# Column tiles 8 to 11 of the state products of batches 0 to 3 from stacked halves, in a fused attention and squared-ReLU kernel

## The chip, the core and the metric

The kernel runs on one core of a Trainium2 chip. The metric is the device time of one execution in microseconds (us); lower is better. Matmuls run on TensorE (PE in the profile, its weight loads PEld), the work beside them on VectorE (DVE), ScalarE (ACT) and GpSimd (POOL). Most transfers are issued by SyncE (SP), some by ScalarE.

## What is computed

For each of 8 batches and 8 heads, 512 tokens and 32 state rows of width 64 read each other by softmax attention; the two results, joined along the rows, go through a feed-forward layer with a squared ReLU.

```python
scores = scale * np.matmul(x, state.transpose(0, 1, 3, 2))       # B 8, H 8, S 512, Ns 32, D 64
a = softmax(scores);   xread = np.matmul(a, state)
scores2 = scale * np.matmul(state, x.transpose(0, 1, 3, 2))
a2 = softmax(scores2); sread = np.matmul(a2, x)
attn = np.concatenate([xread, sread], axis=2)                    # to rows of 512 = 8 heads * 64
h = attn @ w_in                                                  # 512 x 2048
r = np.maximum(h, 0.0); g = r * r
out = g @ w_out                                                  # 2048 x 512
```

## The kernel before

**The products.** For the token rows `xread @ w_in` is not formed in two steps. The kernel first makes, per batch, z = state · w_in (each head's 32 state rows by that head's 64 rows of w_in, for all 2048 columns), and then multiplies the attention weights with z. The 2048 columns are 16 column tiles of 128; two of them make a chunk k (256 columns, k = 0 to 7), four a quarter kq (512 columns, kq = 0 to 3). Heads lie in two groups g of four, each group in two pairs q.

Numbers are split for precision: a float32 operand becomes a high part (a cast on ScalarE to float32r) and a low part (a subtraction on VectorE), and a product is taken as hi·hi + hi·lo + lo·hi, each a matmul of 128x512. The helper `split` (L396) issues both instructions, so they stand at L399 and L404. w_in and w_out come as 64-bit words and are first turned into float32 by `singles` (L408).

**One unit** is a batch and a column tile fc. `up` (L882) multiplies z of the tile with the attention weights into PSUM (`ph`, 6 matmuls), takes the ReLU and the square, and splits the result into `g_hi` and `g_lo`; `down` (L917) multiplies these with the tile's rows of w_out into the four accumulators `po` (12 matmuls). The units run in the order of `PARTS` (L336): batch 0 tiles 0 to 5, batch 1 tiles 0 to 11, batch 0 tiles 6 to 15, batch 1 tiles 12 to 15, then batches 2 to 7 whole and at the end the state rows. So chunk 4 (tiles 8 and 9) is first used by batch 1 in units 14 and 15, chunk 5 in units 16 and 17, and kq = 3 (chunks 6 and 7) from unit 24 on.

**Where z comes from, batches 0 to 3.** Tiles 0 and 1 of batch 0 are made directly (`z_direct`). All else goes through memory and serves four batches at once. There are two ways:

- `z_part(k, g)` (L536): a chunk and a group. Four plain float32 matmuls, contraction 64 (one head each, alternating between the lower and the upper 64 rows of the array), 256 columns, into two PSUM tiles `pz` (L545); two copies on ScalarE into `z_stage` (L528), one store of 512 KB to `zd[k]` on ScalarE's queue. It needs the chunk's two column tiles `wi` and the state `st_z`.
- `z_heads(G, kq, g, q, ...)` (L501): a quarter, a group and a pair of heads, from stacked halves. `w_halves` (L487) lays the high part of a head's 64 rows of w_in above its low part (the two 64-row halves of one tile), by two casts and two subtractions of 64x512; the tile is called `wy` for batches 0 to 3 and lives in the pool tag `raw`. The state's high parts, the same in both halves, and likewise its low parts are the stationary operands. One matmul of 128x512 with the high parts and one with the low ones give a head's product, so four matmuls a call, into two PSUM tiles `py` (L509); two copies (L517) and one store of 512 KB to `zq[G, kq]` on ScalarE's queue. It needs the quarter's four column tiles and the state's halves, made by `z_halves` (L461) from two loads of 256 KB (`sg_raw`) that may begin from unit 8 on. For batches 4 to 7 all z is made in this second way later on (`wz`, `zq_stage`).

`FIRST_KQ = 3` (L319) draws the line: `z_part` makes kq = 0 to 2 (k = 0 to 5), `z_heads` makes kq = 3. `z_fetch(b, k)` (L583) loads a batch's z of a chunk in four pieces of 64 KB on SyncE's queue, and splits it into `z_hi` and `z_lo`. It waits for all stores of its chunk.

The tag `raw` has four buffers. They hold, in turn, the incoming tiles of w_in and w_out (512 KB each), `sg_raw`, the `wy` tiles and the spilled partial sums.

**What sets the order.** No instruction is written in its final place. `Planner` (L50) gets every step with a cost, the buffers it takes, and a due time; due times are passed back from each step to what it needs. It then simulates the engines and takes, on each, the step that can start earliest, and among those the one with the earliest due time. The order that results is issued as it is, and each engine and each queue works through its own list in order. `SHIFTS` (L58) moves the due times of named steps that fall within the first 150 us of the plan. `keep_busy` (L952) adds matmuls on zeros (`idle`) to hold TensorE at its clock, where the plan sees a hole in the first 45 us.

The lines that call the two ways:

```python
    for m in range(2 * FIRST_KQ * NG):
        z_part(*divmod(m, NG))
    z_halves(0)
    for m in range(FIRST_KQ * NG, NFCH // 2 * NG):
        for q in range(NQ):
            z_heads(0, *divmod(m, NG), q, w_halves(0, *divmod(m, NG), q, 0.0), 0.0)
```

Of the kernel before, what the change touches and what calls it, by code (L numbers as in the profile page):

```python
# [49 lines left out]
class Planner:  # L50
# [5 lines left out]
    SLACKS = (2.5,)  # L56
    EARLY = 150.0
    SHIFTS = {  # L58
        ("a_hi", 1): (-7.5, 0.0),
        ("at", 1): (-7.5, 0.12),  # L60
        ("e", 1): (-1.6, 0.19),
        ("g_hi", 1): (-4.1, -0.16),
        ("m", 1): (4.4, 0.0),
        ("out", 1): (0.1, -0.14),
        ("pa", 1): (6.9, 0.0),
        ("po", 2): (3.6, 0.0),
        ("po", 3): (-7.2, 0.22),
        ("po", 7): (-5.3, 0.0),
        ("po", 8): (-0.5, 0.18),
        ("po", 15): (1.4, 0.36),  # L70
        ("po", 18): (-7.2, -0.18),
        ("po", 22): (0.1, 0.0),
        ("po", 23): (-3.4, -0.07),
        ("pz", 1): (-4.8, 0.14),
        ("q", 1): (4.2, 0.0),
        ("q", 3): (-3.9, 0.0),
        ("r", 1): (6.1, 0.0),
        ("st_low", 1): (1.5, 0.18),
        ("wo", 1): (1.1, -0.05),
        ("wo_raw", 1): (-4.5, 0.29),  # L80
        ("wz", 1): (3.2, 0.45),
        ("xt_raw", 1): (-6.0, 0.01),
        ("z_hi", 1): (-0.5, 0.24),
    }

    def __init__(self):
# [203 lines left out]
def memory_attention_then_relu2_ffn(  # L290
# [25 lines left out]
    NT = S // P  # L316
    FW = 256
    NFCH = DF // FW
    FIRST_KQ = 3  # L319
    FPC = FW // P  # L320
    FPQ = 2 * FPC
    GB = P // N
# [26 lines left out]
        r=2, g_hi=2, g_lo=2, os_=3, wof=2, po=4, ph=2, px=2,  # L349
# [5 lines left out]
    def tile_(shape, dtype, name, tag=None):  # L355
        tag = tag or name
        pool = {"po": ps_o, "ph": ps_h, "px": ps_x}.get(tag, sb)
        return Buf(pool, shape, dtype, name, tag, BUFS[tag], hot=tag in ("px", "x_hl"))
# [10 lines left out]
    wi = const.tile([P, NFC, NCC, P], F32, name="wi")  # L369
    wo = [  # L370
        [const.tile([P, FPC, DM], F32R, name=f"{n}{k}") for n in ("wo_hi", "wo_lo")]
        for k in range(NFCH)
    ]
    sd = {
        (b, g): dr.tile([P, S], F32, name=f"sd_{b}_{g}") for b in range(TURNED, PLAIN_X) for g in range(NG)
    }
    zd = [dr.tile([P, NG, HG, FW], F32, name=f"zd_{k}") for k in range(2 * FIRST_KQ)]
    zq = {
        (G, k): dr.tile([P, NG, HG, FPQ * P], F32, name=f"zq_{G}_{k}")
        for G in range(NGB) for k in range(0 if G else FIRST_KQ, NFCH // 2)  # L380
    }
# [70 lines left out]
    st = {}  # L452

    def z_state(G):
        raw = tile_([P, NCC, GB * N], F32, "st_z")
        load(lambda: raw.t.rearrange("p c m -> p (c m)"), lambda: stZ, 256, w=[(raw, 0), (raw, 1)])
        st[G] = raw
# [67 lines left out]
    def z_store(pz, stage, out, keys, part, order):  # L525
        for i in range(2):
            op(
                act(512), lambda e, i=i: nc.scalar.copy(out=part(i), in_=pz[i].t),  # L528
                r=[pz[i]], w=[(stage, i)],
            )  # L530
        load(
            out, lambda: stage.t.rearrange(order), 512,
            r=[(stage, 0), (stage, 1)], w=keys, eng="ACT", issue=0.35, hold=None, land=3.7,
        )

    def z_part(k, g):  # L536
        pz = [tile_([P, NQ, FW], F32, f"pz{i}", "px") for i in range(2)]
        stage = tile_([P, NQ, 2, FW], F32, "z_stage")

        def product(e):  # L540
            for q in range(NQ):
                for i in range(2):
                    own = slice(i * D, (i + 1) * D)
                    cc = g * NQ + q
                    nc.tensor.matmul(  # L545
                        pz[i].t[:, q, :], lhsT=st[0].t[own, cc, :], rhs=wi[own, k * FPC:(k + 1) * FPC, cc, :],
                        start=True, stop=True,
                    )

        op(  # L550
            ("PE", 1.25), product, r=[("wi", k * FPC + i) for i in range(FPC)] + [(st[0], 0), (st[0], 1)], w=pz,
        )
        z_store(pz, stage, lambda: zd[k][:, g].rearrange("p h f -> p (h f)"),
                [("zd", 0, k, g, q) for q in range(NQ)], lambda i: stage.t[:, :, i, :], "p q i f -> p (q i f)")
# [28 lines left out]
    def z_fetch(b, k):  # L583
        raw = tile_([P, NG, FW], F32, "z_raw")
        at = (b % GB) * N
        src = zq[b // GB, k // 2][at:at + N, :, :, (k % 2) * FW:(k % 2 + 1) * FW] if b >= GB or k >= 2 * FIRST_KQ else zd[k][at:at + N]
        for j in range(HG):
# [388 lines left out]
    z_state(0)  # L976
# [5 lines that stand above are left out]
# [3 lines left out]
    spill = {}  # L985
# [96 lines left out]
    for b, lo, hi in PARTS:  # L1082
# [25 lines left out]
        if b == 2 and not z1[0]:  # L1108
            z1[0] = True
            z_halves(1)  # L1110
            for m in range(NFCH // 2 * NG):
                at = begins[2] + m * (begins[GB] - begins[2]) / (NFCH + 2) - 1
# [3 lines left out]
        po = [tile_([P, DM], F32, f"po{t}", "po") for t in range(NT)]  # L1116
        for fc in range(lo, hi):
            k, i = divmod(fc, FPC)
# [4 lines left out]
            z_hi, z_lo = zs[b, k]  # L1123
# [9 lines left out]
            r = [((3 * g, 3 * g + 3), [(z_hi, i), (z_lo, i)] + [(a, g) for a in pairs[b]]) for g in range(NG)]  # L1133
            if u >= 2:
                r = [((0, 3 * NG), r[0][1] + r[1][1][2:])]
# [46 lines left out]
```

## Time and profile before

| what | us |
|---|---|
| median of 3 runs | 668.88 (668.07 to 669.09) |
| profiled execution, device time | 669.25 |
| its span, first to last instruction | 667.5 |
| TensorE busy in it | 660.0 |
| VectorE, ScalarE, GpSimd busy in it | 443.5, 416.5, 90.2 |
| mean granted clock of TensorE | 0.999 |

The span is what the profile shows of an execution; the device time holds 1.75 us more around it. Matmuls are pipelined: a 128x512 matmul shows as about 0.39 us long, but the next begins before it ends, so the cost of a matmul is read from one start to the next. In rows of groups the figures are: line, engine, operation, output <- inputs, shapes, count, then busy time, mean duration in ns, and the idle time of the engine ahead of them. In the answers on one tile the figures are the shortest, the median and the longest duration in ns, and the first and the last start in us.

### The profile page before, as it was taken

How to read it: one execution, taken by the hardware profiler on the slowest of the kernel's cores; microseconds unless marked ns; L12 is line 12 of the kernel's file. 1: busy time of each engine (PE TensorE's matmuls, PEld its weight loads, DVE VectorE, ACT ScalarE, POOL GpSimd, SP SyncE). 2: the span in 40 equal slices, each digit the busy share in tenths (PEclk: the TensorE clock that was granted, in tenths of full speed). 3: DMA queues.
4: the chain of work that ended last, by engine and by line, in shares of the span. 5: the costliest groups of instructions: out<-in, count | busy, mean ns of one | idle time of the engine just before them, and what ended most of it. 6: DMA issues, size and time to landing. Idle time of an engine off the chain costs nothing.

```text
span 667.5 us, 9543 instructions
## 1 busy us (share of the span) xinstructions
PE 660.0 (99%) x3208; PEld 543.9 (81%) x3208; DVE 443.5 (66%) x754; ACT 416.5 (62%) x795; POOL 90.2 (14%) x125
## 2 busy tenths in 40 slices
PE   8999999999999999999999999999999999999997
PEld 6677778888888887888888888888888888988886
DVE  5787887656956798566954694479567945554443
ACT  4998798556668898576643674457556854444331
POOL 1000000033300432021400130013111220000000
PEclk9999999999999999999999999999999999999999
DMA  8989974623623445234130322132223201012101
GB/s 319 353 300 308 274 256 142 234 70 109 221 82 130 143 143 189 68 126 154 53 114 23 104 84 95 31 95 90 96 85 126 64 1 63 1 38 59 32 1 63
DMA packets 43632, 82.41 MB, mean 123 GB/s; under 512 B 7232, under 2 KB 24512, under 8 KB 43584
## 3 DMA queue, kind: packets, MB, share of 16 engines
q1 hardware_dynamic: 38496, 64.38, 29.8%
q10 hardware_dynamic: 5088, 17.44, 6.7%
q8 instruction: 25, 0.41, 0.3%
q14 instruction: 23, 0.19, 0.1%
HBM read 54.00 MB, written 27.79 MB: 123 GB/s over the span
## 4 chain that ended last, share of the span: by engine, by line
PE 92%; DMA 3%; DVE 2%; ACT 2%; issue 1%; SPq 0%; ACTq 0%; DVEq 0%
PE po L930 52%; PE ph L893 28%; PE pr L832 2%; PE pz L509 2%; DMA w_raw<-w_in 2%; PE pq L698 2%; PE pz L545 2%; PE pt L814 1%; DMA wo_raw<-w_out 1%; PE idle L957 1%; PE py L509 1%; PE sq L660 1%; SPq L439 0%; DMA z_raw<-zd 0%; PE pzd L569 0%
## 5 line engine op out<-in xcount | busy, mean ns | idle before, releaser
L930 PE MATMUL po<-wo_hi,g_hi 128*128 128x512 f32 x544 | 213.2, 392 | 0.1
L930 PE MATMUL po<-wo_lo,g_hi 128*128 128x512 f32 x544 | 212.1, 390 | 0.0
L900 ACT ACTIVATE r<-ph 128x512 f32<-128x512 f32 (+1 forms) x144 | 82.7, 575 | 148.9 <-PE ph L893 147.7
L908 DVE TENSOR_TENSOR ph<-ph,r 128x512 f32<-128x512 f32 (+1 forms) x112 | 74.2, 662 | 124.5 <-ACT r L900 124.3
L930 PE MATMUL po<-wo_hi,g_lo 128*128 128x512 f32 x544 | 152.8, 391 | 0.0
L930 PEld LDWEIGHTS po<-wo_hi,g_hi 128*128 128x128 f32 x544 | 102.2, 188 | 22.9 <-ACT g_hi L399 1.1
L930 PEld LDWEIGHTS po<-wo_lo,g_hi 128*128 128x128 f32 x544 | 102.2, 188 | 20.9
L404 DVE TENSOR_TENSOR g_lo<-ph,g_hi 128x512 fp32r<-128x512 f32 (+1 forms) x144 | 94.6, 657 | 33.6 <-ACT g_hi L399 23.6
L930 PEld LDWEIGHTS po<-wo_hi,g_lo 128*128 128x128 f32 x544 | 100.5, 188 | 20.0 <-issue 0.3
L399 ACT CAST g_hi<-ph 128x512 fp32r<-128x512 f32 (+1 forms) x144 | 81.1, 563 | 36.9 <-DVE ph L908 26.3
L893 PE MATMUL ph<-a_hi,z_hi 128*128 128x512 f32 x256 | 101.6, 397 | 0.7 <-DVE g_lo L404 0.7
L893 PE MATMUL ph<-a_hi,z_lo 128*128 128x512 f32 x256 | 99.8, 390 | 0.0
L893 PE MATMUL ph<-a_lo,z_hi 128*128 128x512 f32 x256 | 99.7, 390 | 0.0
L893 PEld LDWEIGHTS ph<-a_hi,z_hi 128*128 128x128 f32 x256 | 48.1, 188 | 12.2 <-DVE g_lo L404 1.3
L893 PEld LDWEIGHTS ph<-a_lo,z_hi 128*128 128x128 f32 x256 | 48.1, 188 | 10.2
L893 PEld LDWEIGHTS ph<-a_hi,z_lo 128*128 128x128 f32 x256 | 48.1, 188 | 9.4 <-issue 0.2
L404 DVE TENSOR_TENSOR z_lo<-z_raw,z_hi 128x512 fp32r<-128x512 f32 x63 | 45.7, 726 | 3.5 <-ACT z_hi L399 3.1
L858 POOL TENSOR_TENSOR sr<-both,low 32x64 f32<-32x64 f32 x64 | 21.6, 337 | 136.5 <-ACT low L850 133.5
L399 ACT CAST z_hi<-z_raw 128x512 fp32r<-128x512 f32 x63 | 39.0, 619 | 1.1 <-DMA z_raw<-zd 0.8
L404 POOL TENSOR_TENSOR xn_hl<-xn_raw,xn_hl 128x512 fp32r<-128x512 f32 x12 | 16.4, 1363 | 171.1 <-ACT xn_hl L399 171.0
L404 DVE TENSOR_TENSOR wz<-wi,wz 64x512 fp32r<-64x512 f32 x32 | 25.0, 780 | 2.2 <-ACT wz L399 1.4
L399 ACT CAST xn_hl<-xn_raw 128x512 fp32r<-128x512 f32 x32 | 19.8, 619 | 9.9 <-PE pr L832 9.0
(152 smaller groups left out, 766.3 us busy)
## 6 DMA issues: line engine op xcount, KB each, us to landing
z_raw<-zq SPq DMA_DIRECT2D x160, 64.0 KB, 2.5
w_raw<-w_in SPq DMA_DIRECT2D x16, 512.0 KB, 6.5
wo_raw<-w_out SPq DMA_DIRECT2D x16, 512.0 KB, 5.1
xn_raw<-xn SPq DMA_DIRECT2D x16, 512.0 KB, 3.3
zq<-zq_stage ACTq DMA_DIRECT2D x16, 512.0 KB, 3.1
xt_raw<-xT SPq DMA_DIRECT2D x15, 512.0 KB, 3.8
zd<-z_stage ACTq DMA_DIRECT2D x12, 512.0 KB, 5.9
z_raw<-zd SPq DMA_DIRECT2D x92, 64.0 KB, 2.5
```

The lines of the kernel that those rows point to most:

```text
L399: act(n, 0.03 if both else 0.0), lambda e: nc.scalar.copy(out=hi(), in_=src()),
L404: lambda e: ENGINE[e].tensor_sub(out=lo(), in0=src(), in1=hi().bitcast(F32)),
L509: nc.tensor.matmul(pz.t, lhsT=halves[G][0](j, g * HG + 2 * q + i), rhs=m.t[:, i].rearrange("p c f -> p (c f)"), start=j == 0, stop=j == 1,)
L545: nc.tensor.matmul(pz[i].t[:, q, :], lhsT=st[0].t[own, cc, :], rhs=wi[own, k * FPC:(k + 1) * FPC, cc, :], start=True, stop=True,)
L660: nc.tensor.matmul(sq.t, lhsT=wide[b].t[:, g].rearrange("p q n -> p (q n)")[:, q * P:(q + 1) * P], rhs=xt.t[:, q, :], start=q == 0, stop=q ...
L698: nc.tensor.matmul(pq.t, lhsT=sp_hl[:, g, q].rearrange("p i n -> p (i n)"), rhs=hl.t[:, i], start=i == 0, stop=i == 1,)
L832: nc.tensor.matmul(pr.t[:, q].rearrange("p i c -> p (i c)"), lhsT=eh.t[:, t, q].rearrange("p i n -> p (i n)"), rhs=hl.t[:, t].rearrange("p ...
L858: nc.gpsimd.tensor_add(out=sr[b // GB][at:at + N, h * D:(h + 1) * D], in0=both.t[i * N:(i + 1) * N, q, i * D:(i + 1) * D], in1=low.t[i * N ...
L893: nc.tensor.matmul(ph.t[:, :width], lhsT=w, rhs=v, start=j == 0, stop=j == len(pairs_) - 1)
L900: act(width), lambda e: nc.scalar.activation(rl.t[:, :width], ph.t[:, :width], AF.Relu),
L908: nc.vector.tensor_mul(out=ph.t[:, :width], in0=ph.t[:, :width], in1=rl.t[:, :width])
L930: nc.tensor.matmul(po[t].t, lhsT=(g[0], g[0], g[1])[j].t[:, t * P:(t + 1) * P], rhs=wo[k][j % 2][:, i, :], start=first and j == 0, stop=la ...
```

## The change

`FIRST_KQ` goes from 3 to 2. `z_part` then makes chunks 0 to 3, and column tiles 8 to 11 (chunks 4 and 5, kq = 2) of batches 0 to 3 go by `w_halves` and `z_heads` into `zq[0, 2]`. The planner's cost for a `z_part` is set from 1.25 to 1.45, and the table `SHIFTS` is replaced by another, so that the whole order of the start is planned anew. The code of the two ways stays as it is.

```diff
     SHIFTS = {
-        ("a_hi", 1): (-7.5, 0.0),
-        ("at", 1): (-7.5, 0.12),
...
-        ("wz", 1): (3.2, 0.45),
-        ("xt_raw", 1): (-6.0, 0.01),
-        ("z_hi", 1): (-0.5, 0.24),
+        ("g_lo", 1): (-0.7, -0.07),
+        ("nm", 2): (7.0, 0.22),
...
+        ("xt_hl", 1): (1.0, -0.14),
+        ("xt_raw", 1): (-0.2, 0.14),
+        ("z_stage", 1): (2.9, -0.4),
     }
...
-    FIRST_KQ = 3
+    FIRST_KQ = 2
...
         op(
-            ("PE", 1.25), product, r=[("wi", k * FPC + i) for i in range(FPC)] + [(st[0], 0), (st[0], 1)], w=pz,
+            ("PE", 1.45), product, r=[("wi", k * FPC + i) for i in range(FPC)] + [(st[0], 0), (st[0], 1)], w=pz,
         )
```

More of the change, by code (lines that the diff above doesn't have):

```diff
@@ L58 @@
     SHIFTS = {
-        ("a_hi", 1): (-7.5, 0.0),
-        ("at", 1): (-7.5, 0.12),
[L61 to L80, printed above, removed]
-        ("wz", 1): (3.2, 0.45),
-        ("xt_raw", 1): (-6.0, 0.01),
-        ("z_hi", 1): (-0.5, 0.24),
+        ("g_lo", 1): (-0.7, -0.07),
+        ("nm", 2): (7.0, 0.22),
+        ("part", 1): (6.4, 0.17),
+        ("po", 1): (1.6, -0.45),
+        ("po", 6): (-1.7, 0.15),
+        ("po", 9): (0.9, 0.37),
+        ("po", 11): (6.9, 0.0),
+        ("po", 16): (0.0, 0.03),
+        ("po", 18): (-1.3, 0.12),
+        ("po", 21): (7.2, 0.06),
+        ("pt", 1): (1.6, -0.24),
+        ("py", 1): (-1.6, 0.0),
+        ("pz", 1): (-4.3, 0.08),
+        ("s", 1): (-1.3, 0.0),
+        ("spill", 1): (-12.5, 0.02),
+        ("st", 1): (-8.8, 0.0),
+        ("wi", 2): (2.7, -0.18),
+        ("wo", 1): (-2.1, 0.17),
+        ("wo_raw", 1): (4.1, 0.0),
+        ("wof", 1): (12.7, 0.05),
+        ("wz", 1): (2.8, 0.34),
+        ("xt_hl", 1): (1.0, -0.14),
+        ("xt_raw", 1): (-0.2, 0.14),
+        ("z_stage", 1): (2.9, -0.4),
     }
```

## The prediction, made before the result

> **What bounds the kernel now.** I read the page first: busy times, the slices, the chain that ended last.
>
> ```profile
> span 667.5 us, 9543 instructions
> PE 660.0 (99%) x3208; PEld 543.9 (81%) x3208; DVE 443.5 (66%) x754; ACT 416.5 (62%) x795; POOL 90.2 (14%) x125
> ...
> PE 92%; DMA 3%; DVE 2%; ACT 2%; issue 1%; SPq 0%; ACTq 0%; DVEq 0%
> ```
>
> TensorE is busy for 99% of the span and 92% of the chain lies on it. So the end is set by three sums: the matmuls that are issued, the idle matmuls that fill holes, and the few real stalls. An engine beside it counts only where it makes one of the last two. The waits of TensorE and the idle fillers say how large those are.
>
> ```profile
> PE sq L660 <- DMA xt_raw<-xT: 1.0, 1, 1.0
> PE idle L957 <- DVE warm L366: 1.0, 1, 1.0
> PE ph L893 <- DVE g_lo L404: 0.7, 1, 0.7
> PE pz L509 <- ACT zq_stage L517: 0.3, 1, 0.3
> PE pzd L569 <- DVE wi L431: 0.3, 1, 0.3
> ...
> L957 PE MATMUL idle<-warm x128: 219/219/314, 1.0 to 37.7; 128*128 128x128 bf16 x128
> ...
> 11.93 1.79 PE idle L957 x32
> 14.78 1.67 PE idle L957 x28
> ```
>
> All stalls together are 3.3 us. The last two rows are from the chain (start, us, what): the largest fillers behind the first scores, 3.5 us. No filler starts after 37.7 us. From there on TensorE is fed almost without a break, and a microsecond of matmul taken out there is a microsecond of the end, as long as what comes next is ready.
>
> **The products that go.** `z_part` runs for chunks k = 0 to 5 and two groups, twelve times; the change leaves k = 0 to 3. The trace shows the twelve as 96 records, eight each. I read two of them, with their neighbours, in the timeline (start, us, instruction):
>
> ```profile
> 57.51 0.40 PE L930 MATMUL po<-wo_hi,g_lo 128*128 128x512 f32 x1
> 57.84 1.13 PE L545 MATMUL pz<-wi,st_z 64*128 64x256 f32 x8
> 58.90 0.50 PE L893 MATMUL ph<-a_hi,z_hi 128*128 128x512 f32 x1
> 59.24 0.40 PE L893 MATMUL ph<-a_hi,z_lo 128*128 128x512 f32 x1
> ...
> 78.22 0.39 PE L930 MATMUL po<-wo_lo,g_hi 128*128 128x512 f32 x1
> 78.53 1.13 PE L545 MATMUL pz<-wi,st_z 64*128 64x256 f32 x8
> 79.60 0.50 PE L893 MATMUL ph<-a_hi,z_hi 128*128 128x512 f32 x1
> 79.94 0.40 PE L893 MATMUL ph<-a_hi,z_lo 128*128 128x512 f32 x1
> ...
> 112.96 0.39 PE L893 MATMUL ph<-a_lo,z_hi 128*128 128x512 f32 x1
> 113.19 0.39 PE L509 MATMUL py<-wy,wo_hi 128*128 128x512 f32 x1
> ...
> 113.87 0.39 PE L509 MATMUL py<-wy,wo_lo 128*128 128x512 f32 x1
> 114.10 1.07 PE L930 MATMUL po<-wo_hi,g_lo 128*128 128x512 f32 x4
> ```
>
> Durations overlap, so I count from start to start. Between the third and the fourth of the last group lie two more `py`. A 128x512 matmul takes one place of (114.10 − 112.96) / 5 = 0.228 us. From 57.51 to 59.24 are 1.73 us, from 78.22 to 79.94 are 1.72; each holds two ordinary places (0.46) beside the `z_part`, which therefore costs 1.27 us: 1.06 inside, and about 0.1 on each side, where the matmul before it and the one behind it take 0.33 and 0.34 instead of 0.23. Four go: 5.08 us. They are the last four of the twelve, after 57 us, where TensorE is fed without holes.
>
> **The products that come.** `z_heads` of batches 0 to 3, now also for quarter kq = 2: two groups by two pairs, each with two tiles of two matmuls: 16 matmuls 128x512, as the `py` rows. 16 × 0.228 = 3.65 us. Net on TensorE: 3.65 − 5.08 = **−1.43 us**.
>
> A rule of the Trainium skill speaks against that saving. By "FP8 and Floating Point Precision" (TensorE Precision Notes) a true FP32 matmul makes four passes, and by "TensorEngine Tiling" (Theoretical Speedup) a contraction of 64 gains up to two by row tiling; so the four 256-column products would stream 4 × 256 × 4 / 2 = 2048 columns, as many as four of 512, and the net would be nothing. The rows above show 1.06 against 0.91 us inside, and by "TensorEngine Tiling" (Key Properties) a change of tiling mode drains the engine, which agrees with the 0.33 and 0.34 at the edges.
>
> **What comes beside TensorE.** Each of the four new `z_heads` needs `w_halves` first: two casts on ScalarE, two subtractions on VectorE.
>
> ```profile
> L399 ACT CAST wy<-wi x8: 602/617/622, 92.2 to 108.6; 64x512 fp32r<-64x512 f32 x8
> L404 DVE TENSOR_TENSOR wy<-wi,wy x8: 685/687/689, 93.0 to 109.7; 64x512 fp32r<-64x512 f32 x8
> L517 ACT COPY yq_stage<-py x8: 579/590/606, 101.5 to 121.4; 128x512 f32<-128x512 f32 x8
> L439 ACTq DMA_DIRECT2D zq<-yq_stage x4: 326/326/333, 103.3 to 122.0; - x4
> ...
> L528 ACT COPY z_stage<-pz x24: 572/590/612, 14.8 to 86.1; 128x512 f32<-128x512 f32 x24
> ...
> 40.00:104.00 64.00, 63.18 (x296) 48.88 (x294) 54.54 (x99) 55.62 (x107) 2.34 (x2) 1.00 0.81 271
> 104.00:150.00 46.00, 46.00 (x215) 38.20 (x214) 28.25 (x48) 30.26 (x59) 7.67 (x12) 1.00 0.46 150
> ```
>
> Eight casts are 4.9 us and eight subtractions 5.5 us, both new. The copies out of PSUM are eight before and after, 0.59 us each; the stores are four of 512 KB before and after, on the same queue (ACT's), and `z_fetch` reads the same 64 KB pieces, from another tensor. So the addition beside TensorE is 10.4 us of work on two engines. In the stretch from 40 to 104 us (columns of the windows: stretch, length, PE, PEld, DVE, ACT, POOL, clock, DMA, GB/s) VectorE is busy 54.5 of 64 and ScalarE 55.6, together 17.9 us free: it fits, but fills 58% of the room. From 104 to 150 both are idle for a third, and what is not urgent can go there: `w_halves` and the loads for kq = 3, whose last store is issued only at 122 us, and the last tiles of w_out. I price the 10.4 us at nothing on the path. Its cover is the matmul stream. If that cover is gone the bounds are, on one side, nothing, and on the other a stall of the kind seen, 0.7 us for `ph` behind `g_lo`, twice: 1.4 us. I keep nothing, since one such stall in 64 us at 86% is what the trace shows.
>
> Two kinds of step move. The stacked state (`sg_raw`, two loads of 256 KB, then two casts and two subtractions) was loaded at 77 us and must come ahead of kq = 2; 512 KB at the 271 GB/s of the row are 1.9 us by which the loads behind it on SP's queue, weights of the next quarter among them, land later. And four more tiles `wy` pass through the four buffers of the tag raw, in which the weight loads stand too; a load that waits there for a `py` product holds back every later load on SP's queue, z pieces included. The trace has that wait already:
>
> ```profile
> SPq L439 <- PE py L509: 7.6, 3, 4.8
> ```
>
> The nearest row bounds it: 7.6 us of queue wait for four `wy` tiles, of which TensorE felt none. With eight tiles in a tighter place it may feel some; that is a rival below. A planner cost of 1.45 in place of 1.25 issues nothing.
>
> **The sum.** The profiled execution took 669.25 us with its span of 667.5; the median of the runs shown is 668.88, 0.37 below. 669.25 − 1.43 = 667.82 for that execution, and **667.4** for a median. About 0.2% (1.34 us) is what a measurement of this kernel can tell from no change: the forecast is barely beyond it, 667.54 being the edge.
>
> **Rival 1: the new order fills the early holes.** Every step of the first 150 us gets another due time, and the start has 3.5 us of fillers and 3.3 us of stalls to win. The 1.0 for the first x and the 1.0 for the memset of the idle operand stand at the very start and stay; of the other 4.8 a better order may win half: 667.4 − 2.4 = 665.0. For it: nothing in the sixteen column tiles forces the holes at 12 to 17 us once z is in hand. Against: the memory queue runs at its fullest there, and any new order can lose as much as it wins.
>
> **Rival 2: z of chunk 4 comes too late (slower).** Before, chunk 4 needed column tiles 8 and 9 and two `z_part`; now both 4 and 5 need tiles 8 to 11, the stacked state, four `w_halves`, eight `py` tiles and four stores.
>
> ```profile
> 57.02 0.68 DVE L431 SCALAR_TENSOR_TENSOR wi<-w_raw,wi 128x512 int32<-128x512 int32 x1
> 86.74 0.33 ACTq L439 DMA_DIRECT2D zd<-z_stage  x1
> 93.48 0.39 PE L893 MATMUL ph<-a_hi,z_hi 128*128 128x512 f32 x1
> 104.46 0.39 PE L893 MATMUL ph<-a_hi,z_hi 128*128 128x512 f32 x1
> ...
> 87.48 0.69 DVE L404 TENSOR_TENSOR z_lo<-z_raw,z_hi 128x512 fp32r<-128x512 f32 x1
> 103.07 0.69 DVE L404 TENSOR_TENSOR z_lo<-z_raw,z_hi 128x512 fp32r<-128x512 f32 x1
> ...
> zd<-z_stage ACTq DMA_DIRECT2D x12, 512.0 KB, 5.9
> zq<-yq_stage ACTq DMA_DIRECT2D x4, 512.0 KB, 3.2
> ```
>
> The last of tiles 8 to 11 is ready at 57.7 (first row). Units 14 and 15, the first users of chunk 4, begin at 93.5 (unit 16, of chunk 5, at 104.5); with 1.4 us saved ahead of them, 92.1. So the whole chain has 34.4 us. For kq = 3 it took, from the first cast (92.2) to the landing of the last store (122.0 + 3.2), 33 us; then comes the fetch and split, for chunk 5 from the store's landing (86.7 + 5.9) to the end of `z_lo` (103.8), 11.1 us. Together 44: at that pace the unit would be 9.7 us late. But that pace was leisurely, since kq = 3 was not due until later; at three quarters of it nothing is late. That is the point from which it decides. Halfway the delay is 4.8 us, of which a held-back `down` of 12 matmuls (12 × 0.228 = 2.7) could fill part: 2.1 us of stall and, with the saving inside, 667.4 + 2.1 = 669.5; with the same stall a second time, before chunk 5, 671.6. I take 670.5. For it: 0.7 us lay between the end of `z_lo` of chunk 5 (103.8) and its use at 104.5, so this place is already tight. Against: chunk 4's z was split (87.5 to 88.2) 5 us ahead of its use, and the due times pull the chain forward.
>
> By "TensorE: Matmul & The Clock Gate" (Part 1) a TensorE idle for about 3.4 us falls to half clock, which would make a long stall dearer; the clock column here is 1.00 throughout, and no run here shows it.
>
> **Rival 3: the saving is given back.** Two more stalls of 0.7 us under the 10.4 us of new conversions, or the rule on passes being right in substance: 667.4 + 1.4 = 668.8, no change. For it, 86% busy on both helpers; against, the room after 104 us, and for the rule the 1.27 us of the rows.
>
> **How the numbers follow.** Forecast (start as good as before to within 1 us): 0.42, which falls about evenly on both sides of the edge, 0.23 faster and 0.19 within 0.2%. Rival 1: 0.22, faster. Rival 2: 0.20, slower. Rival 3: 0.16, of which 0.04 for the rule on passes, within 0.2%. So faster 0.45, within 0.2% 0.35, slower 0.20. The range reaches down to rival 1 at 664.8 and up past rival 2 to 671.0; outside lie the far ends of both, about 0.18 in all.
>
> **What would show it.** In the changed profile: 64 records of `pz` L545 instead of 96, 32 of `py` L509 instead of 16, 16 casts and 16 subtractions of `wy`; the last `z_part` before about 60 us; start-to-start distances of 0.228 at the `py`. If the forecast is right, TensorE's stalls and fillers sum to what they do now, within 1 us, and no wait of `ph` names a `z_lo` or a z transfer. Rival 2 shows as a wait of `ph` behind `z_lo` or `z_hi` between 85 and 110 us, with fetches queued on SP behind `py`. Rival 1 shows as fewer than 128 idle matmuls or shorter stalls before 45 us. The forecast is wrong if the products cost other than 1.27 and 0.228, or if fillers and stalls move by more than the 1.4 us that the products give.

## The result and the profile after

The changed kernel takes 675.20 us (median of 5 runs, 672.78 to 675.40) where the kernel before takes 668.88 (668.07 to 670.26): ratio 1.0087, 95% interval 1.0071 to 1.0103. It is slower by about 6 us, outside the forecast range. Three of its five executions, at a mean granted clock of 0.997, take 675.20 to 675.40 us, and the two at 0.999 and 1.0 take 672.78 and 673.01. The profiled execution is one of the three: it took 675.37 us, and its span is 673.4; the 1.97 us around the span were 1.75 before, so 0.2 us of the difference does not show in the profile.

First the page of the changed kernel: span, busy times, and the shares of the chain that ended last.

```profile
span 673.4 us, 9529 instructions
PE 663.0 (98%) x3196; PEld 546.4 (81%) x3196; DVE 450.6 (67%) x764; ACT 419.9 (62%) x800; POOL 91.5 (14%) x126
...
PE 84%; ACT 7%; DMA 5%; DVE 2%; issue 1%; SPq 0%; ACTq 0%; DVEq 0%
```

Twelve matmuls net are gone, as intended (64 records of `pz` from `z_part` for 96, 32 of `py` for 16, 4 more idle ones), and yet TensorE shows 3.0 us more busy time. TensorE's share of the chain fell from 92% to 84%; ScalarE's rose from 2% to 7%. Next TensorE's waits:

```profile
PE po L929 <- ACT os__871 L945: 2.6, 1, 2.6
PE idle L956 <- DVE warm L365: 1.0, 1, 1.0
PE ph L892 <- DVE g_lo L403: 0.9, 1, 0.9
PE po L929 <- ACT g_hi L398: 0.7, 1, 0.7
```

and the stretches of the prediction with the middle one cut finer (columns: stretch, length, PE, PEld, DVE, ACT, POOL, clock, DMA, GB/s):

```profile
40.00:104.00 64.00, 60.25 (x267) 47.41 (x266) 56.87 (x100) 56.31 (x108) 3.98 (x3) 0.97 0.70 240
...
60.00:80.00 20.00, 17.39 (x70) 13.78 (x69) 18.35 (x31) 18.07 (x35) 0.00 (x0) 0.91 0.78 283
```

From 40 to 104 us TensorE is busy for 60.25 us instead of 63.18, its clock is 0.97 instead of 1.00, and the two helpers have 14.8 us free instead of 17.9. Between 60 and 80 us they have 3.6 us free of 40; in the kernel before, they had 7.3, and TensorE was busy throughout:

```profile
60.00:80.00 20.00, 20.00 (x95) 15.67 (x94) 17.18 (x34) 15.48 (x33) 0.00 (x0) 1.00 0.92 308
```

The longest wait is new: `po` behind `os__871`, a copy on ScalarE. TensorE's timeline at that place (start, us, instruction; in brackets the idle time and what ended it):

```profile
59.34 0.39 PE L929 MATMUL po<-wo_hi,g_hi 128*128 128x512 f32 x1
...
59.79 0.39 PE L929 MATMUL po<-wo_hi,g_lo 128*128 128x512 f32 x1
...
61.83 0.39 PE L929 MATMUL po<-wo_hi,g_lo 128*128 128x512 f32 x1
64.83 0.80 PE L929 MATMUL po<-wo_hi,g_hi 128*128 128x512 f32 x1 [2.61 <-ACT os__871 L945]
65.42 0.63 PE L929 MATMUL po<-wo_lo,g_hi 128*128 128x512 f32 x1
65.85 0.63 PE L929 MATMUL po<-wo_hi,g_hi 128*128 128x512 f32 x1
```

And ScalarE's over the same time:

```profile
58.90 1.14 ACT L398 CAST wo_hi<-sg_raw 128x512 fp32r<-128x512 f32 x2 [1.71 <-DMA sg_raw<-stH]
59.95 0.59 ACT L899 ACTIVATE r<-ph 128x512 f32<-128x512 f32 x1
61.38 0.67 ACT L416 ACTIVATE wo_raw<-wo_raw 128x512 f32<-128x512 f32 x1 [0.85 <-DMA wo_raw<-w_out]
61.95 0.60 ACT L398 CAST wy<-wi 64x512 fp32r<-64x512 f32 x1
62.46 0.57 ACT L398 CAST g_hi<-ph 128x512 fp32r<-128x512 f32 x1
62.94 0.59 ACT L899 ACTIVATE r<-ph 128x512 f32<-128x512 f32 x1
63.55 0.61 ACT L398 CAST wy<-wi 64x512 fp32r<-64x512 f32 x1
64.19 0.59 ACT L945 COPY os__871<-po 128x512 f32<-128x512 f32 x1
```

This is the hand-over of the accumulators. The first part of batch 0 ends with the `down` of 59.34 to 61.83; batch 1's first `down` may not write `po` before batch 0's sums are copied out. The first accumulator is finished by 60.2 (its third matmul starts at 59.79), but ScalarE works through its list in order, stands behind two transfers that have not landed (1.71 and 0.85) and two of the new `wy` casts, and copies only at 64.19. TensorE starts again 3.00 us after its last start, and then its matmuls stand 0.43 us apart instead of 0.228: for about 3.4 us it runs at half clock.

In the kernel before, 5.4 us lay between the last `down` of batch 0 and the first of batch 1: the `z_part` at 57.84, twelve `ph`, and a second `z_part`, of which the timeline shows

```profile
57.25 0.59 ACT L946 COPY os__815<-po 128x512 f32<-128x512 f32 x1
...
61.84 1.13 PE L545 MATMUL pz<-wi,st_z 64*128 64x256 f32 x8
62.90 0.50 PE L930 MATMUL po<-wo_hi,g_hi 128*128 128x512 f32 x1
```

The change takes both products away, and the new order puts the `ph` ahead of the last `down`, so that nothing is left between.

To see the whole, I took every distance of TensorE from one start to the next, subtracted the ordinary place of its kind (the median in the kernel before; a `z_part` 1.06), and summed the rest by stretch of the profiled execution. This is arithmetic on the trace, not a view; all in us. The rest of the span, 5.4 us in both, lies ahead of TensorE's first start and behind its last.

```
kernel     span   places  fillers  lost in 0-40  40-60  60-80  80-120  120-300  from 300
before     667.5  644.7     8.9         3.1      1.2    0.4     1.5      1.2      1.0
after      673.4  644.1    10.1         2.4      0.7    4.5     2.9      2.3      1.0
```

The products give 0.6 in places and 0.8 more in the edges of the four `z_part`, which stood under "lost". The fillers take 1.1 more, the stretch from 60 to 80 us 4.1 (some 1.6 of it the half clock), that from 80 to 120 us 1.3, and short waits after 160 us 1.1.

### The profile page after: what moved, and what is told of

Read it like the earlier page. It is cut to its first block, busy times and chain, and to the rows that moved or that the text cites. A ratio compares the mean times of both kernels' runs of the same rounds, so it can differ in the third digit from the quotient of the medians.

```text
span 673.4 us, 9529 instructions
## 1 busy us (share of the span) xinstructions
PE 663.0 (98%) x3196; PEld 546.4 (81%) x3196; DVE 450.6 (67%) x764; ACT 419.9 (62%) x800; POOL 91.5 (14%) x126
## 4 chain that ended last, share of the span: by engine, by line
PE 84%; ACT 7%; DMA 5%; DVE 2%; issue 1%; SPq 0%; ACTq 0%; DVEq 0%
PE po L929 48%; PE ph L892 26%; DMA w_raw<-w_in 2%; PE pr L831 2%; PE pz L508 2%; PE pq L697 1%; PE pz L544 1%; PE pt L813 1%; DMA wo_raw<-w_out 1%; PE idle L956 1%; ACT wz L398 1%; ACT r L899 1%; DMA xn_raw<-xn 1%; ACT wy L398 1%; DMA zq<-yq_stage 1%
## 5 line engine op out<-in xcount | busy, mean ns | idle before, releaser
L907 DVE TENSOR_TENSOR ph<-ph,r 128x512 f32<-128x512 f32 (+1 forms) x114 | 75.5, 663 | 121.4 <-ACT r L899 121.1
L892 PEld LDWEIGHTS ph<-a_lo,z_hi 128*128 128x128 f32 x256 | 48.2, 188 | 10.2
L892 PEld LDWEIGHTS ph<-a_hi,z_lo 128*128 128x128 f32 x256 | 48.3, 189 | 10.1 <-DVE z_lo L403 0.8
L403 DVE TENSOR_TENSOR z_lo<-z_raw,z_hi 128x512 fp32r<-128x512 f32 x63 | 47.9, 761 | 3.5 <-ACT z_hi L398 3.2
```

The source lines that it names most:

```text
L403: lambda e: ENGINE[e].tensor_sub(out=lo(), in0=src(), in1=hi().bitcast(F32)),
L892: nc.tensor.matmul(ph.t[:, :width], lhsT=w, rhs=v, start=j == 0, stop=j == len(pairs_) - 1)
L907: nc.vector.tensor_mul(out=ph.t[:, :width], in0=ph.t[:, :width], in1=rl.t[:, :width])
```

## The experiments

Each was timed beside runs of the kernel before on the same chip; e1 to e4, e5 to e8, e9 to e12, e13 to e15 and e16 to e18 each share one set of these, and the ratios are to that set. The theories: **T**, the prediction's, TensorE's sum sets the end. **H**: between 57 and 107 us the work in the in-order lists of ScalarE and VectorE sets the pace as much as TensorE does. **A**: the loss is the one uncovered hand-over. **C**: the late load of the stacked state is at the root of it. **R** was formed later: the landings of weight loads, for which those lists wait, set the pace. The letters in the expectations are not all the same: B there, the overfull helpers, is H here; C there is wider in most places, lists in order that wait for transfers, of which R is a part; and in e3, e4 and e11 A is the order at large.

### The products alone, in the order of before

```diff
         def product(e):
+            if k >= 4:
+                for i in range(2):
+                    for q in range(NQ):
+                        nc.tensor.matmul(pz[i].t..., lhsT=wo[0][q][:, i, :P], rhs=wo[0][0][:, i, :],
+                                         start=q == 0, stop=q == NQ - 1)
+                return
```

e15 has the same edit without the loop over `q`: two matmuls in each of the four places instead of four.

> The kernel before, with its order untouched: only the matmuls of the four z_part calls of chunks 4 and 5 are replaced, at their places, by four 128x512 float32r matmuls each, on other data (z of chunks 4 and 5 is then not the reference's). Theory (a z_part costs 1.27 us, four 128x512 matmuls 0.91): 4 x 0.36 = 1.4 us less, 667.4. Rival (only streamed columns count, 2048 against 2048): no difference, 668.9. If the second holds, the exchange itself was mis-priced by 1.4 of the difference between forecast and result.

> The kernel before, in its order, with each z_part of chunks 4 and 5 replaced by two matmuls of 128x512 where e1_exchange had four (z of these chunks not the reference's): 1.27 - 0.46 = 0.81 us of TensorE less in each of four places, 3.25 in all, and nothing else touched. If TensorE's sum sets the end after 37.7 us, as the prediction said: 668.75 - 3.25 = 665.5, 0.995. If the helpers' lists set the pace between 57 and 107 us, the time that is taken out comes back as waits of po and ph, as in e1: 0.999 to 1.004.

Measured: e1 670.37 (668.57 to 672.66), ratio 1.0032 [1.0018, 1.0047]; e15 670.62 (667.53 to 672.64), 1.0026 [1.0009, 1.0044]. Taking 1.43 us or 3.25 us out of TensorE, and nothing else, gives nothing; the time rises by about 2 us (what part half clock has in that is told at the end). T falls. The waits of e15, and its timeline at the longest:

```profile
PE ph L900 <- DVE g_lo L404: 3.4, 2, 2.1
```

```profile
78.79 0.39 PE L900 MATMUL ph<-a_lo,z_hi 128*128 128x512 f32 x1
81.32 0.50 PE L900 MATMUL ph<-a_hi,z_hi 128*128 128x512 f32 x1 [2.15 <-DVE g_lo L404]
81.66 0.49 PE L900 MATMUL ph<-a_hi,z_lo 128*128 128x512 f32 x1
81.94 0.63 PE L900 MATMUL ph<-a_lo,z_hi 128*128 128x512 f32 x1
```

The `g_lo` that it waits for, and in the kernel before the same `g_lo` and the same `ph`:

```profile
80.58 0.69 DVE L404 TENSOR_TENSOR g_lo<-ph,g_hi 128x512 fp32r<-128x512 f32 x1
...
80.31 0.69 DVE L404 TENSOR_TENSOR g_lo<-ph,g_hi 128x512 fp32r<-128x512 f32 x1
81.09 0.46 PE L893 MATMUL ph<-a_hi,z_hi 128*128 128x512 f32 x1
```

In the kernel before, TensorE came to this `ph` at 81.09, and `g_lo` had ended at 81.00: ready in time by 0.1 us. In e15 TensorE comes early and waits for a `g_lo` that ends at 81.27, no earlier than it did before.

### Room for the helpers

The kernel before without the conversions of tiles 8 to 15 of w_out (e7), and the same with the cheaper products of e1 (e8).

```diff
+        first = len(plan.ops)
         singles(lambda: wf.t, lambda: raw.t, [raw], [wf])
         split(lambda: wo[k][0][:, i, :], lambda: wo[k][1][:, i, :], lambda: wf.t, DM, ...)
+        if fc >= 8:
+            for o in plan.ops[first:]:
+                o.run = leave_out
...
-                            rhs=wo[k][j % 2][:, i, :], start=first and j == 0, stop=last and j == 2,
+                            rhs=wo[k if k < 4 else 0][j % 2][:, i, :], start=first and j == 0, stop=last and j == 2,
```

> The kernel before, its order untouched, with the conversions of the tiles 8 to 15 of w_out left out (about 3 us each on ScalarE and VectorE together; the transfers stay, and those products read tile 0 and 1 of w_out instead). It serves as the base of the next run. Both theories: the wait of 0.7 us at 95.5 us, and little else, goes: 667 to 668.

> The same, with the products of chunks 4 and 5 exchanged as in the first experiment. Theory C (the exchange does save 1.4 us of TensorE, and it was lost because ScalarE's and VectorE's lists, waiting for transfers of weights, hold TensorE up between 67 and 98 us): without these conversions the saving reaches the end, 1.0 to 1.5 us less than the run before it. Rival D (the exchange is worth nothing on TensorE, or memory transfers of z hold it): within 0.4 us of the run before it.

Measured: e7 668.30, ratio 0.9995 [0.9984, 1.0006]; e8 667.29, ratio 0.9983 [0.9972, 0.9994]. Between them lie 1.0 us of the 1.43; drawing new sets from the twelve executions of each puts it between 0.5 and 1.7. So the exchange does save TensorE time, and it arrives, at least in good part, once the helpers have less to do; with their full lists (e1) none does.

### The new conversions

The changed kernel without the eight casts and eight subtractions of `wy` for kq = 2.

```diff
+            if (G, kq) == (0, 2):
+                for o in plan.ops[-2:]:
+                    o.run = leave_out
...
-                        rhs=m.t[:, i].rearrange("p c f -> p (c f)"), start=j == 0, stop=j == 1,
+                        rhs=wo[0][0][:, i, :] if (G, kq) == (0, 2) else m.t[:, i].rearrange("p c f -> p (c f)"), ...
```

> The changed kernel with the 8 casts and 8 subtractions of wy for column tiles 8 to 11 left out (the products read another tile, so z of these tiles is not the reference's); order and all else as they are. Rival B (ScalarE and VectorE overfull by these 10.4 us): the waits of TensorE between 55 and 110 us, 4.4 us and a stretch at half clock, fall to 1.5 us or less, and the time falls by 4 us or more, to 671 or less. Theory C (lists in order that wait for transfers): the two casts ahead of the first copy of po go, 1.2 us, but the wait for w_out and the stacked state stays: the time falls by 1 to 3 us, to 672 to 674.

Measured: 671.80 (669.27 to 674.53), ratio 1.0045 [1.0030, 1.0060] for 1.0087: the 10.4 us of conversions cost 2.8 us of the end, with an uncertainty of about 1.4. Some 1 us of it is half clock that comes less often, in 3 of 12 executions instead of 3 of 5: among those at full clock the medians are 670.9 (ratio 1.0035) and 672.9 (1.0060), 1.7 us apart. This is less than the 4 us that was expected if overfull helpers were all of it. The loss from 80 to 120 us falls from 2.9 to 0.6; the wait at the hand-over stays:

```profile
PE po L939 <- ACT os__868 L955: 2.3, 1, 2.3
```

### The hand-over

e2 moves the three copies of `po` on ScalarE ahead of the `wo_raw` and `wy` work in its list. e9 moves the `up` of the next unit on TensorE behind the last `down`, so that six matmuls more lie there, and `r`, the copies and `g_hi` ahead of the casts of the stacked state. e10 is e9 with the sixteen `wy` conversions of kq = 3 about 8 us later. e5 is e2 with the stacked state loaded some 20 us earlier (issued at 32.3 us instead of 53.1), into storage of its own.

```diff
         log = min(plans)[2]
+        copies = [x for x in log if x[3].kind[0] == "os_"][:3]
...
+        moved = [downs[0], copies[0], downs[1], copies[1], downs[2], copies[2], downs[3]]
...
+        front = [up, first("DVE", "z_lo"), relu, downs[0], square, copies[0], hi, downs[1],
+                 copies[1], lo, downs[2], copies[2], downs[3]]
...
+            while wys and wys[0][0] + 8.0 <= x[0]:
+                log.append(wys.pop(0))
...
+        early = [x for x in log if x[2] == "SP" and x[3].bufs and x[3].bufs[0].name == "sg_raw"]
+        log = log[:at] + early + [x for x in log[at:] if not any(x is y for y in early)]
```

(`moved` is of e2 and e5, `front` of e9 and e10, the loop of e10, `early` of e5.)

> The changed kernel, with one edit of its order: the first three copies of the accumulators of batch 0 on ScalarE stand ahead of the wo_raw step and the two wy casts instead of behind them. Theory A (the copies came late because ScalarE's list waited for a transfer and for the new casts; po of batch 1 had to wait 2.6 us and TensorE then ran 3.4 us at half clock): that wait is gone or under 1 us, the clock stays at 1.00 there, and the time falls by 3 to 4.5 us, to 671 to 672. Rival B (ScalarE and VectorE are simply overfull from 55 to 110 us by the 10.4 us of new conversions): the wait returns a few us later at another place, and the time falls by less than 1.5 us, 674 or more.

> The changed kernel with the copies of po moved up, and the stacked state loaded some 15 us earlier into storage that is free until the reads of x, so that ScalarE's casts of it find their data (1.4 us of waiting before). Theory C (between 57 and 105 us ScalarE and VectorE work through lists in order, and each wait of theirs for a transfer reaches TensorE): TensorE's wait behind g_hi at 62 us falls from 1.5 to under 0.5 us, and the time falls by 1 to 2.5 us against the run with the copies moved up alone (674.1), to 671.6 to 673. Rival B (the two engines are simply overfull there): no change beyond 0.7 us, the wait moves on.

> The changed kernel with the hand-over from batch 0 to batch 1 given cover again: the first up-product of unit 6 stays ahead of the last down of batch 0, that of unit 7 goes behind it, and ScalarE makes the three copies of po, with the relu and cast of unit 6 between them, ahead of the casts of the stacked state. Theory A2 (the stall of 2.8 us and the 3.4 us at half clock come from TensorE having nothing between the last down of batch 0 and the first of batch 1): the wait for the copies and the half clock go, 1.36 us of up-products lie in between, and 3 to 4.5 us are saved, 671 to 672. Rival B (ScalarE and VectorE are behind by that much anyway): TensorE waits as long for g_hi or py within the next 15 us, less than 1.5 us saved.

> The same, and the 16 conversions for column tiles 12 to 15 (the third to fifth use of wy, not needed before 110 us) stand about 8 us later in the lists of ScalarE and VectorE. By the run without wy conversions the waits between 88 and 107 us, 2.4 us in the changed kernel, hang on the load of these two engines. Theory B (load): these waits fall to under 1 us and 1.5 us are saved against the run before it, 669.5 to 671. Theory C (waits for transfers of weights in those lists): no change beyond 0.7 us. If both edits work, the time comes near that of the kernel before.

Measured: e2 674.13, ratio 1.0087 [1.0072, 1.0103]; e5 677.40, 1.0131 [1.0110, 1.0152]; e9 673.70, 1.0079 [1.0066, 1.0092]; e10 674.25, 1.0087 [1.0073, 1.0101]. The wait for the copy goes, and others take its place. First e2, then e9:

```profile
PE po L937 <- ACT g_hi L406: 2.1, 2, 1.5
PE py L516 <- ACT yq_stage L524: 1.4, 2, 0.9
```

```profile
PE py L524 <- ACT yq_stage L532: 1.5, 2, 1.0
...
PE ph L908 <- DVE g_lo L419: 0.9, 1, 0.9
```

The loss between 60 and 80 us stays at 4.6 us in e2, 4.5 in e5, 4.3 in e9 and e10 (4.5 in the changed kernel). In these four profiles there is no half clock in it: other waits have come in the place of the one. In e9 the row is

```profile
60.00:80.00 20.00, 17.16 (x71) 12.46 (x70) 18.30 (x31) 17.90 (x34) 0.00 (x0) 1.00 0.79 282
```

Among executions at full clock e2 stands at 1.0089 and e9 at 1.0073 (four of five each), no better than the changed kernel at 1.0060 (two of five). A falls in its simple form: the one wait can be taken away, its time cannot. H, too, expected more of e10, 1.5 us, and it gained nothing over e9. C found no support: e5 lies about 3 us above e2, where C expected 1 to 2.5 less and H no change; but e5 loses 0.8 us at unit 4 already, where its early loads stand in the way of others, so it doesn't settle C alone.

### Which order, which line

Two tables, no table (`SHIFTS = {}`), and both values of `FIRST_KQ`; the planner's cost of a `z_part` is 1.45 with the new table and 1.25 otherwise. e3 has the old table and e12 none, at `FIRST_KQ = 2`; e4 has the new table and e11 none, at 3.

```diff
-    FIRST_KQ = 3
+    FIRST_KQ = 2
...
-    SHIFTS = {
-        ("a_hi", 1): (-7.5, 0.0),
...
+    SHIFTS = {}
```

> Only FIRST_KQ goes to 2; the planner's cost of 1.25 and the table of shifts stay those of the kernel before, and the order is planned from them. Theory A (the loss is in how this order fell out, a hand-over without cover, not in the stacked products): another order with the same products, whose time may lie on either side, 666 to 674, and where it loses, the waits of TensorE name other places than the copies of po. Rival B (the stacked products of chunks 4 and 5 cost the early stage more than it has): again 672 or more, with waits of TensorE above 4 us between 55 and 110 us.

> The new table of shifts and the cost of 1.45, but FIRST_KQ stays 3: the products of the kernel before in yet another order. Theory A (an order decides, not the products): a time that differs from 668.9 by more than 1 us either way, likely longer, as this table was not made for these products. Rival B (the products decide): within 1 us of 668.9.

> The kernel before with an empty table of shifts: its products, in the order that the planner gives by itself. Theory A (orders that were not picked lose several us through waits): 672 to 690. Rival (the order matters little): within 1.5 us of 668.5.

> FIRST_KQ at 2, an empty table and the planner's cost at 1.25: the pair of the run before. If the stacked products themselves fit the early stage, it lies within 3 us of that run on either side; if they load the stage beyond what it has, it is 3 us or more slower.

```
median, us (ratio)    old table           no table          new table
FIRST_KQ = 3          668.88 (1)          677.34 (1.0130)   676.88 (1.0123)
FIRST_KQ = 2          689.21 (1.0324)     685.33 (1.0253)   675.20 (1.0087)
```

An order tuned for the other structure is no better than none (676.88 beside 677.34, 689.21 beside 685.33); e3 lies far above the 666 to 674 that was expected of it. A table of its own is worth 8.5 us to `FIRST_KQ = 3` and 10.1 to 2. With no table the change costs 8.0 us, with each structure's own 6.3. So a table made for the old structure is not the reason for the loss: the change is slower in both fair pairs. But each cell is a single order, and orders of one structure lie 8 to 14 us apart, so the pairs don't say how much of the 6 us is structure and how much the order that was found; that a better order exists for `FIRST_KQ = 2` is not excluded.

### Do the costs add up?

The changed kernel with the edits of e6 and e9 together (e13), and with that of e7 too (e14).

> The changed kernel with both single edits that gained at all: the eight casts and eight subtractions of the stacked tiles of kq = 2 left out (the products read a tile of w_out in their place, so z of chunks 4 and 5 is not the reference's), and the hand-over from batch 0 to batch 1 covered by an up unit, as in e9_cover. If the two costs are separate and add up as they did one by one (1.0087 to 1.0045, and 1.0087 to 1.0079): 1.0037, 671.2 us. If the stalls that e9 still had between 60 and 80 us come from the load of the two helper engines, they go with the conversions, and all that the profile of the change put down to stall and half clock (4.4) comes back as well: 675.2 - 4.4 - 2.8 = 668.0, 0.999. Rival: the stalls there belong to the order itself and to late transfers: 671 to 673, with a loss of about 4 us between 60 and 80.

> The same, and the conversions of column tiles 8 to 15 of w_out left out too (down uses tiles 0 and 1 there, so the output is not the reference's): the fewest conversions on ScalarE and VectorE of all kernels here. If these two engines' load between 57 and 107 us is what kept the 1.43 us of TensorE from arriving, this kernel is about as far below the kernel before as the exchange without these conversions was (0.9983, 667.3), or 1.4 below at best (0.9979). If the new order itself costs what is left (fillers and stalls of the first 40 us, stalls between 60 and 80 us), it stays above: 1.001 to 1.004.

Measured: e13 670.17 (669.38 to 672.09), ratio 1.0023 [1.0012, 1.0035]; e14 669.44, ratio 1.0016 [1.0005, 1.0027]. The two edits give 0.64%, 4.3 us, together, where one by one they gave 0.42 and 0.08. None of the twelve executions of e13 is at half clock, which is part of it. The stretch that was worst in the changed kernel, now in e13 (its profiled execution is the longest of its runs):

```profile
60.00:80.00 20.00, 19.51 (x85) 15.52 (x84) 14.46 (x25) 15.32 (x29) 0.00 (x0) 1.00 0.84 291
```

TensorE is busy for 19.5 of the 20 us, not 17.4, and the helpers have 10.2 us free, not 3.6: with the conversions gone, the cover holds there. From 80 to 104 us this execution of e13 still has TensorE idle for 2.3 us, of which 1.5 are two waits of `ph` behind `g_lo`. e14 has hardly a stall left between 40 and 104 us,

```profile
40.00:104.00 64.00, 63.09 (x292) 50.53 (x291) 50.29 (x88) 50.42 (x96) 3.99 (x3) 1.00 0.73 246
```

and still stands at 1.0016, where e8, with the same products in the old order and the same conversions of w_out left out, stands at 0.9983. That difference, 0.33% or 2.2 us, goes with the new order: fillers of 10.1 us for 8.9, and 1.1 us more lost between 120 and 300 us.

So the 0.87% can be walked: cheaper products with helpers that have room −0.17% (e8), the new order +0.33% (e14), the conversions of w_out +0.07% (e13), the sixteen new conversions and the bare hand-over +0.64%; each step is uncertain by 0.1 to 0.2%, so the 0.07 is not told from nothing. The last step holds the half clock too: among executions at full clock the changed kernel is at 1.0060, so some 0.3 of the 0.64 is half clock.

### What holds the lists: work or landings

The kernel before (e16), e1 (e17) and e15 (e18) with loosened loads: the stacked state in storage of its own, so that one tile fewer passes the tag raw, and three spill stores behind two loads of w_in on SyncE's queue instead of between them.

```diff
+        spills = [x for x in queue if x[3].kind[0] == "spill"][1:4]
...
+        log = head + spills + tail
...
+            raw.make = lambda: sr[0]
```

> The kernel before with its loads loosened and nothing else: the stacked state of batches 0 to 3 is loaded into storage of its own (that of the state rows' sums, unused until the end), so one tile fewer passes through the four buffers of the tag raw, and three spill stores go behind two loads of w_in on SyncE's queue instead of between them. Conversions, products and the orders of all engines stay. In the profiles so far unit 12 starts 5.5 us after a w_in tile has landed (75.50 and 81.09 here, 76.30 and 81.84 in e1, 75.78 and 81.32 in e15) and unit 15 7.0 us after a w_out tile (89.58 and 96.60; 90.88 and 97.88; 91.11 and 98.10). Theory R, the landings of weight loads set the pace: both landings come 1 us or more earlier, the stall of 0.86 before unit 15 goes, 667.9 or a little less, 0.998 to 0.999. Theory H, the helpers' load sets it: 1.000.

> The same loosened loads with the cheaper products of e1_exchange (z of chunks 4 and 5 not the reference's). All conversions are made. Theory R: what e1 lost (1.0032) behind late landings goes, and the 1.43 us of TensorE arrive at least in part: 0.996 to 0.999. Theory H: as e1, 1.002 to 1.004, since the helpers have the same work.

> The same loosened loads with the products of e15_half_product, 3.25 us less of TensorE (z of chunks 4 and 5 not the reference's). Theory R: the start of unit 12 is still 5.5 us after a landing, but the landing is 1 us or more earlier, and that of the w_out tile 2 us or more; so at least 1 to 2 of the 3.25 us arrive: 0.994 to 0.999. Theory H: as e15, 1.001 to 1.004.

Measured: e16 668.99 (668.12 to 673.00), ratio 1.0020 [1.0004, 1.0036]; e17 669.68, 1.0026 [1.0009, 1.0042]; e18 671.66 (670.16 to 673.50), 1.0052 [1.0035, 1.0069]. The times are nearer to H than to R, and e18 fits neither. The starts in the profiles say why (us of the span; the landing is that of the w_out tile whose conversion stands in ScalarE's list ahead of the `g_hi` that unit 15 waits for):

```
             unit 12  unit 14   landing   unit 15   landing to unit 15
before        81.09    93.48     89.58     96.60      7.02
e1            81.84    93.80     90.88     97.88      7.00
e15           81.32    94.39     91.11     98.10      6.99
e16           81.03    93.20     89.14     96.30      7.16
e17           81.16    92.94     89.29     96.47      7.18
e18           80.57    91.90     89.53     96.58      7.05
e7 (left out) 81.23    93.40       -       95.73       -
e8 (left out) 80.74    92.61       -       94.88       -
```

The loosened loads bring the w_in tile forward (it landed at 75.5 to 76.3, now at 73.3 to 74.3), and unit 12 no longer waits: e18 is 1.57 us ahead of the kernel before at units 13 and 14. But the w_out tile lands at 89.1 to 89.5, at most 0.4 ahead of the kernel before, and unit 15 begins 7.0 to 7.2 us after it in all six, while unit 14 begins anywhere between 91.9 and 94.4. ScalarE in the kernel before,

```profile
89.67 0.66 ACT L424 ACTIVATE wof<-wo_raw 128x512 int32<-128x512 uint8 x1 [0.87 <-DMA wo_raw<-w_out]
...
92.25 1.27 ACT L399 CAST wy<-wi 64x512 fp32r<-64x512 f32 x2
...
95.26 0.56 ACT L399 CAST g_hi<-ph 128x512 fp32r<-128x512 f32 x1
```

and in e18, where TensorE comes earlier:

```profile
89.61 0.68 ACT L434 ACTIVATE wof<-wo_raw 128x512 int32<-128x512 uint8 x1 [0.77 <-DMA wo_raw<-w_out]
...
92.24 1.26 ACT L409 CAST wy<-wi 64x512 fp32r<-64x512 f32 x2
...
95.23 0.57 ACT L409 CAST g_hi<-ph 128x512 fp32r<-128x512 f32 x1
```

The same list at the same times: a landing, then 5.6 us of instructions one behind the other, eight of them conversions, then `g_hi`, then `g_lo` on VectorE, then TensorE. So H and R are each a part of it: the landing sets when the list goes on, and the conversions in it set how long it takes. Where the conversions are left out (e7, e8), unit 15 follows unit 14 by 2.3 us and a saving on TensorE passes through. In e18 the wait is 2.25 us, unit 16 begins 1.58 us late, half clock follows in the profile, and all six executions have a mean clock below 0.9985: more time is lost than was taken out.

No version here beats the kernel before with all of its work done.

## Why the prediction was wrong, point by point

**The products: right.** The twelve `z_part` of before sum to 13.00 us from start to start inside, the eight of after to 8.52, 1.08 and 1.07 each; the added `py` stand 0.227 apart, the last four 0.23 to 0.26. The rule of the Trainium skill by which both ways would stream alike ("FP8 and Floating Point Precision", TensorE Precision Notes, with "TensorEngine Tiling", Theoretical Speedup) leaves no saving; e8 against e7 measured one of 1.0 us, so the rows decide.

**"A microsecond of matmul taken out there is a microsecond of the end": this step failed.** The page's 99% and the chain's 92% were read as one bound. In the kernel before, TensorE and the helpers' lists were level at several places (0.1 us at 81.09, a stall of 0.86 at 95.5), and the `z_part` stood there as cover that needed little from the helpers. The clause "as long as what comes next is ready" was written, but not applied to the places where the products stood: the `g_lo` that ended at 81.00 for a `ph` at 81.09 was in the trace.

**"I price the 10.4 us at nothing on the path": failed too.** They cost 2.8 us by e6, some 1 us of it as half clock. The upper bound of 1.4 was too low: 86% busy over 64 us says that there is room, not where, and a list that stands behind a landing cannot use the room that it has. The stall of 0.7 us behind `g_lo` was read as the size that such a thing may have; it was the sign that the lists were already the bound there.

**The cover named for it, "the matmul stream", was what the change took away.** At the hand-over 5.4 us of matmuls became none, at a price of 2.77 us of stall and about 1.6 of half clock in the profiled execution. Putting six matmuls back there (e9) did not win that time; it did so only together with fewer conversions (e13).

**The order.** Fillers and losses before 40 us went together from 12.0 to 12.5 us: rival 1, holes filled, did not come. The 2.2 us between e14 and e8 lie in fillers and at places after 120 us that the prediction did not look at.

**Rival 2 had the right sign and mostly the wrong place.** Its mark, a wait of `ph` behind `z_lo` between 85 and 110 us, is there and 0.2 us long. Unit 14, the first to use chunk 4, begins at 100.58 instead of 93.48, and that is mostly by the plan: unit 13 is 2.3 us late by then (91.73 for 89.40), and 32 matmuls of held-back `down` stand between the two instead of 12. Rival 3 named the mechanism, stalls under the new conversions, with too small a size and no place.

What stays open: how the 4.5 us from 60 to 80 us in the changed kernel divide between landings and work (no run brought the landings of that stretch forward without crowding others), and why e1 lies 1.1 us above the kernel before in its executions at full clock: its w_out tile lands 1.3 us later in the profile, and why it does was not traced.

## What to carry to other kernels

Where the matrix engine is busy for 99%, look ahead of each matmul that is to go at what starts behind it, and how long before that its inputs were ready; if that is less than the time to be taken out, only that much can come back there. Judge room on a helper engine by its list between a landing and the next hand-over, not by its mean over a stage. An order tuned for one structure can be worth more than the change that is compared under it, so compare structures with no table and each with its own.

## What the runs showed of the hardware

**Half clock after waits of about 1 to 3 us.** After the wait of 2.61 us in the changed kernel the stretch reads

```profile
65.00:68.40 3.40, 3.40 (x9) 2.71 (x10) 3.31 (x6) 3.33 (x7) 0.00 (x0) 0.52 0.74 260
```

and after that of 2.15 us in e15

```profile
81.70:85.00 3.30, 3.30 (x10) 2.52 (x9) 3.22 (x8) 2.95 (x7) 0.00 (x0) 0.52 0.80 185
```

"TensorE: Matmul & The Clock Gate" (Part 1) in the Trainium skill names an idle window of about 3.4 us, on a window that runs freely. The waits here are shorter than that; a window that runs freely would fit that the half clock comes only in some executions of one kernel, which no run here tests.

Nor is 2 us a threshold. In the kept profiles half clock comes with every wait of TensorE of 2.1 us or more after 40 us, but in e12 also one of 1.03 us (from 110.28 us) and in e4 one of 1.61 (from 193.59, for 6.8 us), while waits of 1.66 in e1 and of 1.53 in e2 and e5 pass at full clock.

A mean clock below 0.9985 stands in 3 of 5 executions of the changed kernel (median 675.4, the other two 672.9), 5 of 12 of e1 (672.1 and 669.2), 7 of 12 of e15 (670.9 and 668.6), 3 of 12 of e6, 4 of 12 of e17, all 6 of e18, and 1 of 28 of the kernel before beside e15. In the first three the executions with it take 2.4 to 2.9 us more, of which the half clock itself, 3.41 us long in the profiles of the changed kernel and of e15, explains at most 1.7; so it comes with longer waits or causes others, and which of the two was not traced. It also stands in 3 of 11 of e16, whose profile, at full clock, shows no wait of 1 us after 40 us. This is part of why less work on TensorE took longer. At full clock alone e1 takes 669.2 us beside 668.0 of the kernel before, and e15 668.6 beside 668.2: neither the 1.43 nor the 3.25 us arrive even there.
